# Scores and products with v share three PSUM slots; the softmax denominator is applied on the way out of PSUM; q and k load through a ring of three

## The chip, the cores and the metric

One kernel, one launch, on one core of a Trainium2 chip. The metric is device time in microseconds, so less is better. One core has five engines that run side by side and wait for each other by semaphores: TensorE (PE, its weight loads are shown apart as PEld), VectorE (DVE), ScalarE (ACT), GpSimd (POOL) and SyncE (SP), which here issues all DMAs.

## What is computed

Attention with rotary positions over 4 batches of 8 heads, 576 positions, 64 dimensions a head, and two feed-forward layers behind it, of 2304 tokens, 512 to 2048 to 512 channels. The first has a rational function between its two products, the second a squared relu.

```python
q_rot, k_rot = (rotate(q), rotate(k))
scores = scale * np.matmul(q_rot, k_rot.transpose(0, 1, 3, 2))
scores = scores - np.max(scores, axis=-1, keepdims=True)
attn = np.exp(scores)
attn = attn / (np.sum(attn, axis=-1, keepdims=True) + 1e-09)
x = np.matmul(attn, v)
...
h = x @ w_in
P = a[0] + a[1] * h + a[2] * h * h + a[3] * h * h * h
Q = 1.0 + np.abs(b[0]) * np.abs(h) + np.abs(b[1]) * h * h
x = (P / (Q + 1e-06)) @ w_out
...
h = np.maximum(x @ w2_in, 0.0)
out = (h * h) @ w2_out
```

## The kernel before

The kernel has two stages. The attention works on 16 pairs of heads, and a pair in five units (c = 0 to 4) of 128 query rows of each of its two heads (the last unit holds the 64 rows that are left). The feed-forward stage, called MoE in the code, then runs 160 steps, each 12 products into `ph` (two splits of x by two splits of the weights, three of the four, for each of four slices) and 12 products into the output banks.

**A pair, engine by engine.** `rope` loads q and k of a pair into `raw` (one DMA for q, one for k). POOL multiplies by the table of cosines and sines, adds the two halves, ACT casts the high part (`qh`, `kh`), POOL subtracts to get the low part (`ql`, `kl`). `scores` makes 12 matmuls for a unit, six for each head, into the two PSUM tiles `sc0` and `sc1` (two banks each). DVE takes each tile out with one instruction that writes `e` and the row minimum of the negated scores (`neg`), which frees the tile. ACT takes the exponential and sums the row (`sums`). PE transposes `e` into two PSUM banks (`tr`), from which ACT and DVE copy to `et`. `av` multiplies `et` by v, in two parts of 256 and 320 query columns, into two PSUM banks (`y`). DVE copies each part into the SBUF tile `t`. `normalise` adds 1e-9 to the sums on DVE, takes the reciprocal and a transpose there, sends the row to DRAM (`dr`) and back as three broadcast loads (`rr`). POOL multiplies `t` by `rr` into `xf`, the input of the feed-forward stage.

**What sets the order.** Each operation is a task with an engine, a cost in nanoseconds and a rank (position in the program plus an offset by kind from the table `RANK`). `Plan.run` simulates the engines with these costs and, each time an engine is free, takes the task with the smallest rank among those that are ready; a bonus `BOND` keeps tasks of one PE layout together. The instructions are then written in that order, so each engine works through a fixed list, and its first waiting instruction holds up all behind it. A task depends on another through keys (`r`, `w`). In the kernel before, the key of a score tile is `("sc", h)`, the one of a product with v `("y", i)`:

```python
self.pe(6 * 131, (n, "qk"), product, r=rd, w=[("sc", h) for h in range(2)], mode="rows")
```

so a unit's 12 score matmuls wait until both tiles of the unit before have been taken out. The eight PSUM banks are `sc0` and `sc1` (two each), `tr` (two) and `y` (two); in the feed-forward stage the last four are the output banks, and the first four `ph`.

The weights of the feed-forward stage are unpacked in chunks, each a DMA, three instructions on DVE (`wy`), two on ACT (`wx`, and the cast to `wsi`, `wso`, `wli` or `wlo`) and one on POOL; six chunks are unpacked while the attention still runs.

Of the kernel before, what the change touches and what calls it, by code (L numbers as in the profile page):

```python
# [9 lines left out]
F32 = mybir.dt.float32  # L10
# [4 lines left out]
ALU = mybir.AluOpType  # L15
# [4 lines left out]
P = 128  # L20
# [20 lines left out]
TRANSPOSE = 60  # L41
# [52 lines left out]
class Plan:  # L94
# [7 lines left out]

    LATENCY = {"dma": 2000}

    def __init__(self):
        self.tasks, self.writer, self.readers, self.base = [], {}, {}, 0
        self.order = set()

    def add(self, eng, ns, rank, fn, r=(), w=(), after=(), mode="", shared=False):
# [15 lines left out]
        self.order.update((d, i) for d in late)  # L125

# [6 lines left out]
    def run(self, trace=True):  # L133
# [13 lines left out]
        self.seq = [0] * len(tasks)  # L147
# [27 lines left out]
SWITCH, BOND = 160, 77.2  # L175

RANK = {"const": -332.5, "load": -240.8, "rope": 66.7, "add": -190.1, "hi": 466.7, "lo": -245, "wrap": 223.7,
        "spread": -16.2, "vload": -62.2, "qk": 7.4, "max": -58.9, "exp": 101.9, "dup": 356, "tr": -448.9,
        "trc": 381.9, "eth": -54.1, "av": 438, "t": 370.8, "inv": 804, "fin": -323.6, "wload": 966,
        "wx": 467.4, "wy": 51.1, "wh": 143.9, "wl": -174.2, "xh": 554.7, "xl": 53.4, "h": -384.7,  # L180
        "chain": -206.7, "gh": -85.2, "gl": 575.4, "o": 40.3, "evac": -273.4, "out": -182.5}


class Ops:
# [5 lines left out]
    def pe(self, ns, rank, fn, r=(), w=(), mode="full"):  # L190
        self.plan.add("pe", ns, rank, fn, r, w, mode=mode)
# [16 lines left out]
    def tt(self, eng, n, rank, out, a, b, op, r=(), w=(), ps=False):  # L208
        ns = 150 + 2.2 * n if eng == "pool" else 68 + 1.042 * n
        self.plan.add(eng, ns, rank, lambda: self.engine(eng).tensor_tensor(ap(out), ap(a), ap(b), op=op), r, w,  # L210
                      shared=not ps)
# [6 lines left out]
    def ts(self, eng, n, rank, out, a, s0, s1, op0, r=(), w=(), ns=None, ps=False, **kw):  # L218
        ns = ns or (327 + 0.833 * n if eng == "pool" else 68 + 0.522 * n)
        self.plan.add(eng, ns, rank, lambda: self.engine(eng).tensor_scalar(  # L220
            ap(out), ap(a), ap(s0), ap(s1), op0=op0, **{k: ap(x) for k, x in kw.items()}), r, w, shared=not ps)
# [15 lines left out]
class Attention(Ops):  # L237


    def __init__(self, nc, plan, early, late, scores, banks, dram, qk, v, tables, ident, xf):  # L240
# [3 lines left out]
        self.sc, self.tr, self.y = scores.ring(2, [P, 2, 512], F32, "sc"), banks[:2], banks[2:]  # L244
        self.ny = 0
        self.tab = early.tile([P, 2, S], F32, "tab")
        self.raw = early.tile([P, 4, S], F32, "raw")
# [7 lines left out]
        self.t = late.tile([P, S], F32, "t")  # L255
        self.rr = late.tile([P, S], F32, "rr")
        self.dr = [dram.tile([32, 4, 32], F32, name=f"dr{i}") for i in range(2)]

    def constants(self):
        for i, cols in enumerate((slice(0, KCUT), slice(KCUT, S))):  # L260
            self.dma((40 * i, "const"), self.tab[:, :, cols], self.tables_ap[:, :, cols], w=[("tab", i)], ns=900)
        self.dma((90, "const"), self.ident, self.ident_ap, w=["ident"])

    def rope(self, p):
        raw, b, at = self.raw, p % 2, 9 * (p - 1)
# [29 lines left out]
    def scores(self, p, c):  # L295
# [11 lines left out]
        def product():  # L307
            for i in range(3):
                for j in range(2):
                    for h, (rows, m, terms) in enumerate(jobs):  # L310
                        w, k = terms[i]
                        self.mm(self.sc[h][m, j, 0:288], w[rows], k[rows, 288 * j:288 * j + 288], i == 0, i == 2)

        self.pe(6 * 131, (n, "qk"), product, r=rd, w=[("sc", h) for h in range(2)], mode="rows")

    def unit(self, p, c):
# [9 lines left out]
        for h, rows, i, col in [(0, every, 0, c), (1, every, 1, 5 + c)] if c < 4 else [(h, slice(64 * h, 64 * h + 64), 1, 4) for h in range(2)]:  # L326

            self.ts("dve", 2 * 288, (n + h, "max"), e[rows, i].rearrange("p (j k) -> p j k", j=2), self.sc[h][rows, :, 0:288],
                    -SCALE, None, ALU.mult, op1=ALU.min, accum_out=self.neg[b][rows, col:col + 1], ns=760, ps=True,
                    r=[("sc", h), "scores"], w=[("neg", b, col, h), ("e", slot, h)])  # L330
# [56 lines left out]
    def av(self, p, part):  # L387
        n = (256, 320)[part]
        b = p % 2
        at = 9 * p + 5 * part  # L390
        y = self.y[self.ny % len(self.y)]
        yk = ("y", self.ny % len(self.y))
        self.ny += 1
# [4 lines left out]
        def product(js):  # L398
            for j in js:
                for h in range(2):  # L400
                    kc, slot = (4 * h + j, 4 * h + j) if j < 4 else (8, 8 + h)
                    self.mm(y[64 * h:64 * h + 64, 0:n], self.vst[b][:, slot], self.et[part][b][:, kc, :], j == 0, j == 4)

        for i, js in enumerate(AVCUT):
            self.pe((5 + 1.667 * n) * len(js), (at + 0.5 * i, "av"), lambda js=js: product(js),
                    r=keys + [("v", b), "early"], w=[yk], mode="columns")
        self.take("dve", n, (at, "t"), self.t[:, 256 * part:256 * part + n], y[:, 0:n], r=[yk], w=[("t", part)])

    def normalise(self, p):
        b = p % 2  # L410
        at = (9 * p, "inv")
        r, rt, dr, rr = self.r[b], self.rt[b], self.dr[b], self.rr
        self.ts("dve", 32, at, r, self.sums[b], 1e-9, None, ALU.add,
                r=[("sum", b, i) for i in range(9)] + [("sums", b)], w=[("r", b)])
        self.plan.add("dve", 270, at, lambda: self.nc.vector.reciprocal(ap(r), ap(r)), w=[("r", b)])
        self.plan.add("dve", 100, at, lambda: self.nc.vector.transpose(out=ap(rt), in_=ap(r)), r=[("r", b)], w=[("rt", b)])
# [3 lines left out]
        for h, first, src, n in ((0, 0, 0, S), (1, 0, S + 64, 512), (1, 512, S, 64)):  # L420
            self.dma(at, rr[64 * h:64 * h + 64, first:first + n], row[src:src + n].unsqueeze(0).to_broadcast([64, n]),
                     r=[("dr", b)], w=[("rr", h, first)])
        bb, hp = divmod(p, NHP)
# [18 lines left out]
class Weights(Ops):  # L442
# [15 lines left out]
    def chunk(self, i, rank):  # L458
# [7 lines left out]
        self.dma(at("wload"), self.raw, self.chunks[i], r=[("xf", 1)] if i < WFIRST else [], w=[raw], ns=1500)  # L466
# [9 lines left out]
class Moe(Ops):  # L476
    def __init__(self, nc, plan, early, late, hidden, banks, xf, weights, a, b, out):
# [12 lines left out]
        self.ps_o = banks  # L490
        self.before = {("o", i): (("tr", "y")[i // 2], i % 2) for i in range(4)}
# [23 lines left out]
    def split_x(self, b, dm, at):  # L515
# [3 lines left out]
        pairs = {("xf", NHP * t + dm) for t in range(STARTS[b] // S, (STARTS[b] + n - 1) // S + 1)}  # L519
# [3 lines left out]
    def unit(self, i):  # L523
# [51 lines left out]
        for dm in range(NDM):  # L575
# [6 lines left out]
            was = [("xf", NHP * t + dm) for t in range(B)] if m == g == 0 else []  # L582
# [119 lines left out]
```

## Time and profile before

| | us |
|---|---|
| median of 3 runs | 1116.99 |
| lowest, highest run | 1111.1, 1119.37 |
| the profiled execution, its own time | 1115.98 |
| its span in the trace | 1114.2 |
| first score matmul of the second pair (pair 1) | 33.15 |
| first score matmul of the last pair (pair 15) | 274.92 |
| first product into `ph` | 297.92 |

A stretch of the trace is read by the busy time of each engine in it, by what ended the idle time of an engine, and by the granted clock of TensorE as a share of its full 2.4 GHz. PE's busy time is modelled and counts matmuls that wait in its pipeline, so a busy PE isn't PE at its peak.

### The profile page before, as it was taken

How to read it: one execution, taken by the hardware profiler on the slowest of the kernel's cores; microseconds unless marked ns; L12 is line 12 of the kernel's file. 1: busy time of each engine (PE TensorE's matmuls, PEld its weight loads, DVE VectorE, ACT ScalarE, POOL GpSimd, SP SyncE). 2: the span in 40 equal slices, each digit the busy share in tenths (PEclk: the TensorE clock that was granted, in tenths of full speed). 3: DMA queues.
4: the chain of work that ended last, by engine and by line, in shares of the span. 5: the costliest groups of instructions: out<-in, count | busy, mean ns of one | idle time of the engine just before them, and what ended most of it. 6: DMA issues, size and time to landing. Idle time of an engine off the chain costs nothing.

```text
span 1114.2 us, 17891 instructions
## 1 busy us (share of the span) xinstructions
PE 1061.9 (95%) x6752; PEld 901.6 (81%) x6752; DVE 794.3 (71%) x1487; ACT 621.8 (56%) x1187; POOL 535.3 (48%) x431
## 2 busy tenths in 40 slices
PE   4998889899889999999999999999999999999998
PEld 3666666666678888888888889888888888888887
DVE  5779888877699888997998899863254446444434
ACT  4667767766668876775766677553443224223221
POOL 4867887872267877877886768320020002001000
PEclk9989989989989999999999999999999999999999
DMA  5344443331001111111110200230021003000002
GB/s 165 119 146 137 128 149 121 111 120 37 23 19 39 53 43 58 36 41 39 57 39 20 76 1 20 76 114 20 1 76 58 20 23 110 1 20 1 35 35 102
DMA packets 26823, 69.19 MB, mean 62 GB/s; under 512 B 6384, under 2 KB 10608, under 8 KB 26736
## 3 DMA queue, kind: packets, MB, share of 16 engines
q1 hardware_dynamic: 26736, 68.04, 19.7%
q8 instruction: 53, 0.87, 0.3%
q14 instruction: 34, 0.28, 0.1%
HBM read 63.05 MB, written 4.98 MB: 61 GB/s over the span
## 4 chain that ended last, share of the span: by engine, by line
PE 87%; DVE 8%; issue 2%; DMA 1%; ACT 1%; POOL 1%; SPq 0%; DVEq 0%; ACTq 0%; POOLq 0%
PE bank L234 42%; PE ph L234 35%; PE sc L234 6%; DVE e L220 4%; PE bank L372 3%; DVE et L385 1%; DMA raw<-in_qk 1%; DVE r L220 1%; POOL raw L210 0%; ACT e L200 0%; DVE wy L215 0%; SPq L231 0%; DMA cols<-in_b 0%; DVE xl L210 0%; POOL ql L210 0%
## 5 line engine op out<-in xcount | busy, mean ns | idle before, releaser
L234 PE MATMUL ph<-xh,wsi 128*128 128x464 f32 (+1 forms) x680 | 199.1, 374 | 4.5 <-DVE g L215 4.5
L234 PE MATMUL bank<-gh,wso 128*128 128x464 f32 (+1 forms) x680 | 197.6, 372 | 0.0
L198 ACT CAST gh<-g 128x464 fp32r<-128x464 f32 (+1 forms) x160 | 92.0, 577 | 153.1 <-PE bank L234 147.7
L234 PE MATMUL bank<-gh,wlo 128*128 128x464 f32 (+1 forms) x600 | 174.3, 371 | 0.0
L234 PE MATMUL ph<-xh,wli 128*128 128x464 f32 (+1 forms) x600 | 174.0, 371 | 0.0
L210 DVE TENSOR_TENSOR gl<-g,gh 128x464 fp32r<-128x464 f32 (+1 forms) x80 | 53.9, 674 | 150.1 <-ACT gh L198 150.0
L234 PEld LDWEIGHTS ph<-xh,wsi 128*128 128x128 f32 x680 | 128.2, 189 | 21.4 <-ACT tt L200 4.8
L234 PEld LDWEIGHTS bank<-gh,wso 128*128 128x128 f32 x680 | 127.6, 188 | 14.8
L220 DVE TENSOR_SCALAR_CACHE_REDUCE e<-sc 128x576 f32<-128x576 f32 (+1 forms) x160 | 115.5, 751 | 26.9 <-PE sc L234 22.7
L200 ACT ACTIVATE e<-e,neg 128x576 f32<-128x576 f32 x144 | 110.9, 773 | 39.5 <-DVE e L220 39.4
L234 PE MATMUL ph<-xl,wsi 128*128 128x464 f32 (+1 forms) x340 | 127.1, 374 | 0.5 <-DVE xl L210 0.5
L234 PE MATMUL bank<-gl,wso 128*128 128x464 f32 (+1 forms) x340 | 126.5, 372 | 0.0
L234 PEld LDWEIGHTS ph<-xh,wli 128*128 128x128 f32 x600 | 112.6, 188 | 13.3
L234 PEld LDWEIGHTS bank<-gh,wlo 128*128 128x128 f32 x600 | 112.6, 188 | 12.9
L210 POOL TENSOR_TENSOR gl<-g,gh 128x464 fp32r<-128x464 f32 (+1 forms) x80 | 103.1, 1290 | 24.9 <-ACT gh L198 20.1
L234 PE MATMUL bank<-gl,wlo 128*128 128x464 f32 (+1 forms) x300 | 111.6, 372 | 0.0
L234 PE MATMUL ph<-xl,wli 128*128 128x464 f32 (+1 forms) x300 | 111.4, 371 | 0.0
L210 POOL TENSOR_TENSOR u<-u,ab 128x464 f32<-128x464 f32 (+1 forms) x80 | 100.1, 1254 | 3.3
L234 PE MATMUL bank<-et,vst 128*64 128x256 f32 (+1 forms) x640 | 100.4, 440 | 0.9 <-DVE et L385 0.9
L210 DVE TENSOR_TENSOR xf<-bank,xf 128x464 f32<-128x464 f32 (+1 forms) x120 | 74.4, 635 | 34.9 <-PE bank L234 34.0
L234 PE MATMUL sc<-kh,qh 64*128 64x288 f32 (+1 forms) x320 | 60.6, 379 | 37.7 <-DVE e L220 25.1
L200 ACT ACTIVATE tt<-ph 128x464 f32<-128x464 f32 (+1 forms) x80 | 44.3, 555 | 91.0 <-DVE g L210 81.6
(68 smaller groups left out, 2007.9 us busy)
## 6 DMA issues: line engine op xcount, KB each, us to landing
raw<-in_qk SPq DMA_DIRECT2D x30, 576.0 KB
rawi<-in_wi SPq DMA_DIRECT2D x32, 512.0 KB
rawo<-in_wo SPq DMA_DIRECT2D x32, 512.0 KB
vst<-in_v SPq DMA_DIRECT2D x16, 320.0 KB
out<-xf SPq DMA_DIRECT2D x12, 232.0 KB
rr<-dr SPq DMA_DIRECT2D x16, 144.0 KB
rr<-dr SPq DMA_DIRECT2D x16, 128.0 KB
out<-xf SPq DMA_DIRECT2D x8, 228.0 KB
```

Of the source, the lines that this page charges most:

```text
L198: self.nc.scalar.copy(ap(out), ap(src))
L200: self.nc.scalar.activation(ap(out), ap(src), func, **{k: ap(x) for k, x in kw.items()})
L210: self.plan.add(eng, ns, rank, lambda: self.engine(eng).tensor_tensor(ap(out), ap(a), ap(b), op=op), r, w, shared=not ps)
L220: self.plan.add(eng, ns, rank, lambda: self.engine(eng).tensor_scalar(ap(out), ap(a), ap(s0), ap(s1), op0=op0, **{k: ap(x) for k, x in kw. ...
L234: self.nc.tensor.matmul(ap(out), ap(w), ap(x), start=start, stop=stop)
L372: self.nc.tensor.transpose(ap(self.tr[i])[0:src.shape[1], 64 * k:64 * k + 64], src[rows], ap(self.ident)[rows, rows])
L385: self.plan.add("dve", 68 + 1.042 * n, rank, lambda: self.nc.vector.tensor_copy(ap(out), ap(src)), r, w)
```

## The change

Three things change in the attention, and the order of nearly everything with them. First, PSUM: `sc0`, `sc1` and a third tile of two banks (`bank2`, which holds what were the two `y` banks) are three equal slots. A score task takes any two (`grab`), DVE's eviction gives one back (`drop`). A product with v takes one for both of its halves, and gives it back when DVE has read it. The planner hands out the slots as it goes, and may hold an engine idle for up to 800 ns for a task of smaller rank. Second, `av` now needs `rr`: DVE multiplies the product in PSUM by `rr` straight into `xf`, so that the copies to `t` and POOL's multiplication go away, and 1e-9 is added on ACT and not on DVE. `av` comes in three pieces for each part as before, but all of it is placed after the pair's reciprocal, so in the pair that follows. Third, `raw` is a ring of three tiles for q and k, not one tile for each. In the feed-forward stage a planner's delay of 130 ns between PE tasks falls away, so the order of its products changes too, from groups of three to groups of twelve. Number, shape and operands of the products are the same.

```diff
-    def add(self, eng, ns, rank, fn, r=(), w=(), after=(), mode="", shared=False):
+        self.where, self.slots, self.patient = {}, {}, 0
+    def add(self, eng, ns, rank, fn, r=(), w=(), after=(), mode="", shared=False, grab=(), drop=(), only=None):
...
+        vacant, last = dict.fromkeys(range(NSLOT), 0.0), {}
+        def able(i):
+            grab, _, only = self.slots.get(i, ((), (), None))
+            if not grab:
+                return ready_at[i]
+            times = sorted(t for s, t in vacant.items() if only is None or s == only)
+            return max(ready_at[i], times[len(grab) - 1]) if len(times) >= len(grab) else math.inf
-            start, eng = min((max(free[e], min(ready_at[i] for i in q)), e) for e, q in open_.items() if q)
-            i = min((i for i in open_[eng] if ready_at[i] <= start),
-                    key=lambda i: (tasks[i][2] - BOND * (tasks[i][5] == mode), i))
+            wait = {i: max(0, able(i) - start) for i in open_[eng]}
+            i = min((i for i, t in wait.items() if t <= HOLD * (i < self.patient)),
+                    key=lambda i: (tasks[i][2] - BOND * (tasks[i][5] == mode) + PULL * wait[i], i))
+            start += wait[i]
...
+            for x in grab:
+                s = min((s for s in vacant if only is None or s == only), key=lambda s: (vacant[s], s))
+                del vacant[s]
+                self.where[x] = s
...
+            for x in drop:
+                s = self.where[x]
+                vacant[s], last[s] = end + CROSS, i
...
-                wait = 0 if (i, u) in self.order else self.LATENCY.get(eng) or (SAME if same else CROSS)
+                wait = 0 if (i, u) in self.order else self.LATENCY.get(eng) or (SAME * (eng != "pe") if same else CROSS)
...
-RANK = {"const": -332.5, "load": -240.8, "rope": 66.7, "add": -190.1, "hi": 466.7, "lo": -245, "wrap": 223.7,
...
+HOLD, PULL = 800, 0.2958
+RANK = {"on": -34.47, "const": 59.32, "load": 145.37, "rope": 96.23, "add": 57.15, "hi": 268.98,
...
-        self.sc, self.tr, self.y = scores.ring(2, [P, 2, 512], F32, "sc"), banks[:2], banks[2:]
...
+        self.ps, self.tr = scores.ring(NSLOT - 1, [P, 2, 512], F32, "sc") + [banks[2]], banks[:2]
...
-        self.raw = early.tile([P, 4, S], F32, "raw")
+        self.raw = early.ring(NRAW, [P, 2, S], F32, "raw")
...
+            i = (2 * p + j) % NRAW
+            raw, (hi, lo) = self.raw[i], parts[j]
...
-        self.pe(6 * 131, (n, "qk"), product, r=rd, w=[("sc", h) for h in range(2)], mode="rows")
+                        self.mm(self.slot(("sc", p, c, h))[m, j, 0:288], w[rows], k[rows, 288 * j:288 * j + 288], i == 0, i == 2)
+        keys = [("sc", p, c, h) for h in range(2)]
+        self.pe(6 * 131, (n, "qk"), product, r=rd, w=keys, mode="rows", grab=keys, after=self.before)
+        self.before = keys[:1]
+    def slot(self, key):
...
-                    r=[("sc", h), "scores"], w=[("neg", b, col, h), ("e", slot, h)])
+                    r=[key, "scores"], w=[("neg", b, col, h), ("e", slot, h)], drop=[key])
...
+        yk = ("y", p, part)
+        rr = [("rr", b, 0, 0), ("rr", b, 1, 0), ("rr", b, 1, 512)]
+        r, only = ([], NSLOT - 1) if p == NPAIR - 1 else (["scores"], None)
         keys = [("m", c, r) for c in ((0, 1), (2, 3, 4))[part] for r in range(2)] + [("c", r) for r in range(2)]
...
-            self.pe((5 + 1.667 * n) * len(js), (at + 0.5 * i, "av"), lambda js=js: product(js),
-                    r=keys + [("v", b), "early"], w=[yk], mode="columns")
-        self.take("dve", n, (at, "t"), self.t[:, 256 * part:256 * part + n], y[:, 0:n], r=[yk], w=[("t", part)])
+            self.pe((5 + 1.667 * n) * len(js), (at + AVSTEP * (3 * part + i), "on" if i else "av"), lambda js=js: product(js),
+                    r=keys + [("v", b), "early", *rr] + r, w=[yk], mode="columns", grab=[yk] * (i == 0), only=only)
+        bb, hp = divmod(p, NHP)
+        first = 256 * part
+        self.tt("dve", n, (at + 5 * part, "fin"), self.xf[:, hp, bb * S + first:bb * S + first + n],
+                Ref(lambda: ap(self.slot(yk))[:, 0, 0:n]), self.rr[b][:, first:first + n], ALU.mult,
+                r=rr + [yk] + r, w=[("xf", p, part)], ps=True, drop=[yk])
...
-        self.ts("dve", 32, at, r, self.sums[b], 1e-9, None, ALU.add,
-                r=[("sum", b, i) for i in range(9)] + [("sums", b)], w=[("r", b)])
...
+        self.act(32, at, r, self.sums[b], func=AF.Identity, bias=self.eps, sb=True,
+                 r=[("sum", b, i) for i in range(9)] + [("sums", b), "eps"], w=[("r", b)])
+        self.plan.add("dve", 370, at, lambda: self.nc.vector.reciprocal(ap(r), ap(r)), w=[("r", b)])
+        self.plan.add("dve", 130, at, lambda: self.nc.vector.transpose(out=ap(rt), in_=ap(r)), r=[("r", b)], w=[("rt", b)])
...
-        self.tt("pool", S, (9 * p, "fin"), self.xf[:, hp, bb * S:bb * S + S], self.t, rr, ALU.mult,
-                r=[("rr", 0, 0), ("rr", 1, 0), ("rr", 1, 512), ("t", 0), ("t", 1)], w=[("xf", p)])
...
-                if c == 1:
-                    self.av(p, 0)
+            self.normalise(p)
+            self.av(p, 0)
             self.av(p, 1)
-            self.normalise(p)
...
-        self.ps_o = banks
...
+        self.ps_o = banks[:2] + [banks[2][:, i] for i in range(2)]
...
-        banks = [ps.tile([P, 512], F32, name=f"bank{i}") for i in range(4)]
+        banks = [ps.tile(s, F32, name=f"bank{i}") for i, s in enumerate([[P, 512]] * 2 + [[P, 2, 512]])]
```

DVE in the middle of the attention: evictions of score tiles (`e,neg<-...`), copies to `et`, unpacking of weights (`wy`), and the work on sums and products. Before, in a row:

```order
L385 COPY et01_105<-bank0_64 128x2x64
L385 COPY et01_105<-bank1_65 128x2x64
L220 TENSOR_SCALAR e3_95,neg1_97<-sc0_123 64x576
L220 TENSOR_SCALAR e3_95,neg1_97<-sc1_124 64x576
L385 COPY et11_107<-bank1_65 128x8x64
L385 COPY t_108<-bank2_66 128x256
L385 COPY t_108<-bank3_67 128x320
L220 TENSOR_SCALAR e0_92,neg0_96<-sc0_123 128x576
L220 TENSOR_SCALAR e0_92,neg0_96<-sc1_124 128x576
L220 TENSOR_SCALAR wy_70<-rawo_72 128x512
L220 TENSOR_SCALAR r1_101<-sums1_99 128x32
```

The same place of a pair in the changed kernel:

```order
L253 TENSOR_SCALAR e2_93,neg0_95<-bank2_66 128x576
L253 TENSOR_SCALAR e2_93,neg0_95<-sc0_125 128x576
L253 TENSOR_SCALAR e3_94,neg0_95<-sc1_126 128x576
L253 TENSOR_SCALAR e3_94,neg0_95<-bank2_66 128x576
L428 COPY et00_103<-bank1_65 128x8x64
L253 TENSOR_SCALAR e0_91,neg0_95<-sc0_125 64x576
L253 TENSOR_SCALAR e0_91,neg0_95<-sc1_126 64x576
L428 COPY et00_103<-bank0_64 128x2x64
L428 COPY et00_103<-bank1_65 128x2x64
L243 TENSOR_TENSOR xf_67<-bank2_66,rr1_108 128x256
L428 COPY et10_105<-bank1_65 128x8x64
L463 RECIPROCAL r0_99<-r0_99 128x32
```

The copies to `t` and the addition to the sums are gone, a product with `rr` has come, the slots rotate, and the reciprocal stands right ahead of the next pair's first evictions.

POOL in the middle of the attention, before: the product by the table (`raw<-raw,tab`), the addition, the low parts, a chunk of weights and the product `xf<-t,rr`.

```order
L210 TENSOR_TENSOR raw_114<-raw_114,tab_113 128x1152
L210 TENSOR_TENSOR wsi1_74<-wy_70,wsi1_74 128x512
L210 TENSOR_TENSOR raw_114<-raw_114 128x576
L210 TENSOR_TENSOR raw_114<-raw_114,tab_113 128x1152
L210 TENSOR_TENSOR xf_68<-t_108,rr_109 128x576
L210 TENSOR_TENSOR ql1_87<-raw_114,qh1_86 128x576
L210 TENSOR_TENSOR raw_114<-raw_114 128x576
```

The changed kernel, one pair on POOL:

```order
L243 TENSOR_TENSOR ql0_118<-raw0_114,qh0_117 128x576
L262 MEMSET sums0_97 128x32
L243 TENSOR_TENSOR kl0_120<-raw1_115,kh0_119 128x576
L243 TENSOR_TENSOR raw0_114<-raw0_114,tab_113 128x1152
L243 TENSOR_TENSOR raw0_114<-raw0_114 128x576
L243 TENSOR_TENSOR raw1_115<-raw1_115,tab_113 128x1152
L243 TENSOR_TENSOR raw1_115<-raw1_115 128x576
```

`xf` has left POOL, and the buffer `raw0` that `ql0` has read is loaded anew and used two instructions later.

PE at the end of the attention, before: the last transposes, the products with v of the last pair (`vst1`), and the first products of the feed-forward stage.

```order
L372 MATMUL bank0_64<-ident_91,e3_95 64x64
L372 MATMUL bank1_65<-ident_91,e3_95 128x64
L234 MATMUL bank3_67<-et11_107,vst1_90 64x320 x10
L234 MATMUL ph0_3636<-xh0_3703,wsi0_73 128x464 x2
L234 MATMUL ph0_3636<-xl0_3704,wsi0_73 128x464
```

The changed kernel there:

```order
L415 MATMUL bank0_64<-ident_90,e3_94 64x64
L415 MATMUL bank1_65<-ident_90,e3_94 128x64
L268 MATMUL bank2_66<-et10_105,vst0_121 64x320 x2
L268 MATMUL bank2_66<-et01_104,vst1_89 64x256 x10
L268 MATMUL bank2_66<-et11_106,vst1_89 64x320 x10
L268 MATMUL ph0_3646<-xh0_3691,wsi0_72 128x464 x2
L268 MATMUL ph0_3646<-xl0_3692,wsi0_72 128x464
```

Both parts of the last pair's product with v, which now need that pair's `rr`, stand together ahead of the feed-forward stage.

## Rows read from the trace of the kernel before

**Rows 1.** Windows: busy us (and instructions) of each engine, granted clock, DMA share.

```profile
core 0: us, PE busy (x) PEld busy (x) DVE busy (x) ACT busy (x) POOL busy (x), PEclk, DMA share, GB/s
33.20:274.90 241.70, 217.00 (x2553) 152.86 (x2551) 201.35 (x512) 169.43 (x377) 175.74 (x115) 0.92 0.39 122
340.00:700.00 360.00, 360.00 (x1720) 322.06 (x1719) 324.44 (x513) 256.59 (x445) 272.84 (x245) 1.00 0.13 40
```

**Rows 2.** Timeline of PE: first score matmuls of pair 1 and of pair 15.

```profile
33.15 0.51 PE L234 MATMUL sc<-kh,qh 64*128 64x288 f32 x4
34.12 0.65 PE L234 MATMUL bank<-et,vst 128*64 128x256 f32 x4
...
274.92 0.53 PE L234 MATMUL sc<-kh,qh 64*128 64x288 f32 x4
```

**Rows 3.** Chain that ended last, 33.2 to 274.9, by engine and line.

```profile
by line: PE bank L234 26.2%; PE sc L234 24.0%; DVE e L220 15.2%; PE bank L372 13.7%; issue 6.0%; DVE et L385 5.2%; DVE r L220 3.0%; ACT e L200 1.8%; DVE wy L215 1.4%; ACT et L198 1.0%; DVE r L415 0.7%; DVE wy L220 0.6%; ACT kh L198 0.4%; AC
```

**Rows 4.** Waits, 33.2 to 274.9: total us, times, longest.

```profile
PE sc L234 <- DVE e L220: 21.3, 41, 1.9
...
DVE e L220 <- PE sc L234: 15.1, 25, 1.9
```

**Rows 5.** Timeline of DVE and PE around one unit's scores.

```profile
107.95 0.76 DVE L220 TENSOR_SCALAR_CACHE_REDUCE e<-sc 128x576 f32<-128x576 f32 x1
...
108.77 0.40 PE L234 MATMUL sc<-kh,qh 64*128 64x288 f32 x1 [0.85 <-DVE e L220]
...
109.45 0.52 PE L234 MATMUL sc<-kh,qh 64*128 64x288 f32 x3 [0.28 <-DVE e L220]
```

**Rows 6.** Groups of POOL by shape, 33.2 to 274.9: busy us, mean ns, idle before.

```profile
L210 POOL TENSOR_TENSOR raw<-raw,tab 128x1152 f32<-128x1152 f32 x26 | 69.1, 2665 | 18.6 <-DMA raw<-in_qk 18.4
L210 POOL TENSOR_TENSOR raw<-raw 128x576 f32<-128x576 f32 x27 | 39.4, 1472 | 0.4
L210 POOL TENSOR_TENSOR xf<-t,rr 128x576 f32<-128x576 f32 x14 | 20.4, 1459 | 23.1 <-DVE t L385 21.0 <-DMA rr<-dr 1.6 <-DVE r L415 0.6
L210 POOL TENSOR_TENSOR kl<-raw,kh 128x576 fp32r<-128x576 f32 x14 | 20.2, 1442 | 5.3 <-ACT kh L198 5.3
L210 POOL TENSOR_TENSOR ql<-raw,qh 128x576 fp32r<-128x576 f32 x14 | 19.9, 1418 | 9.0 <-ACT qh L198 9.0
L210 POOL TENSOR_TENSOR wsi<-wy,wsi 128x512 fp32r<-128x512 f32 x3 | 3.8, 1279 | 0.0
```

**Rows 7.** Timeline of SP and POOL: two raw loads issued, the first one used.

```profile
174.65 1.72 SPq L231 DMA_DIRECT2D raw<-in_qk  x2
...
178.41 2.65 POOL L210 TENSOR_TENSOR raw<-raw,tab 128x1152 f32<-128x1152 f32 x1 [2.40 <-DMA raw<-in_qk]
```

**Rows 8.** Groups of DVE by shape, 33.2 to 274.9.

```profile
L385 DVE COPY et<-bank 128x512 f32<-128x512 f32 x28 | 19.3, 690 | 13.4 <-PE bank L372 10.8 <-ACT e L200 2.2
L220 DVE TENSOR_SCALAR r<-sums 128x32 f32<-128x32 f32 x14 | 14.7, 1047 | 2.8 <-ACT e L200 2.7
...
L385 DVE COPY t<-bank 128x320 f32<-128x320 f32 x14 | 6.8, 487 | 1.1
...
L385 DVE COPY t<-bank 128x256 f32<-128x256 f32 x14 | 5.9, 419 | 0.2
```

**Rows 9.** The page's groups: the nearest product of a PSUM bank and SBUF.

```profile
L210 DVE TENSOR_TENSOR xf<-bank,xf 128x464 f32<-128x464 f32 (+1 forms) x120 | 74.4, 635 | 34.9 <-PE bank L234 34.0
```

**Rows 10.** Timeline of SP and POOL: the reciprocals' way through DRAM, one pair.

```profile
198.26 0.57 SPq L231 DMA_DIRECT2D dr<-rt  x1
200.30 2.46 SPq L231 DMA_DIRECT2D rr<-dr  x3
...
204.79 1.42 POOL L210 TENSOR_TENSOR xf<-t,rr 128x576 f32<-128x576 f32 x1 [1.06 <-DMA rr<-dr]
```

**Rows 11.** Timeline of DVE, SP and PE at the end of the attention.

```profile
291.54 0.18 DVE L220 TENSOR_SCALAR r<-sums 128x32 f32<-128x32 f32 x1 [0.27 <-ACT e L200]
...
292.38 0.56 SPq L231 DMA_DIRECT2D dr<-rt  x1
...
294.75 3.24 PE L234 MATMUL bank<-et,vst 128*64 128x320 f32 x20 [0.93 <-DVE et L385]
297.92 0.69 PE L234 MATMUL ph<-xh,wsi 128*128 128x464 f32 x2
```

More of the change, by code (lines that the diff above doesn't have):

```diff
@@ L40 @@
 KCUT = 288
-TRANSPOSE = 60
+TRANSPOSE = 62
+NSLOT = 3
+AVSTEP = 1.5
+NRAW = 3
 ROPE = {(0, 0): "pool", (0, 1): "dve", (1, 0): "dve", (1, 1): "dve"}
@@ L125, in add @@
         self.order.update((d, i) for d in late)
+        if grab or drop:
+            self.slots[i] = (grab, drop, only)
     def barrier(self, fn, w):
@@ L174 @@
 SAME, CROSS = 130, 180
-SWITCH, BOND = 160, 77.2
-RANK = {"const": -332.5, "load": -240.8, "rope": 66.7, "add": -190.1, "hi": 466.7, "lo": -245, "wrap": 223.7,
[L178 to L181, printed above, removed]
+HOLD, PULL = 800, 0.2958
+SWITCH, BOND = 160, 58.5
+RANK = {"on": -34.47, "const": 59.32, "load": 145.37, "rope": 96.23, "add": 57.15, "hi": 268.98,
+        "lo": -35.36, "wrap": 223.7, "spread": -16.2, "vload": 194.98, "qk": 1.33, "max": -47.2,
+        "exp": 61.91, "dup": 356, "tr": -110.97, "trc": -329.26, "eth": -8.01, "av": 145.83, "t": 370.8,
+        "inv": 1.98, "fin": -54.52, "wload": 951, "wx": 502.88, "wy": 99.07, "wh": -102.22, "wl": -100.64,
+        "xh": 325.05, "xl": 106.51, "h": -619.65, "chain": -139.29, "gh": -154.06, "gl": 943.18, "o": 135.54,
+        "evac": -499.48, "out": -89.96}
 class Ops:
@@ L188, in __init__, with pe @@
         self.nc, self.plan = nc, plan
-    def pe(self, ns, rank, fn, r=(), w=(), mode="full"):
-        self.plan.add("pe", ns, rank, fn, r, w, mode=mode)
+    def pe(self, ns, rank, fn, r=(), w=(), mode="full", **kw):
+        self.plan.add("pe", ns, rank, fn, r, w, mode=mode, **kw)
     def act(self, n, rank, out, src, r=(), w=(), func=AF.Copy, sb=False, extra=0, **kw):
@@ L216, in stt, with ts @@
             ap(out), ap(a), ap(s), ap(b), op0=op0, op1=op1), r, w, shared=not ps)
-    def ts(self, eng, n, rank, out, a, s0, s1, op0, r=(), w=(), ns=None, ps=False, **kw):
+    def ts(self, eng, n, rank, out, a, s0, s1, op0, r=(), w=(), ns=None, ps=False, drop=(), **kw):
         ns = ns or (327 + 0.833 * n if eng == "pool" else 68 + 0.522 * n)
         self.plan.add(eng, ns, rank, lambda: self.engine(eng).tensor_scalar(
-            ap(out), ap(a), ap(s0), ap(s1), op0=op0, **{k: ap(x) for k, x in kw.items()}), r, w, shared=not ps)
+            ap(out), ap(a), ap(s0), ap(s1), op0=op0, **{k: ap(x) for k, x in kw.items()}), r, w, shared=not ps,
+                      drop=drop)
     def copy(self, eng, n, rank, out, src, r=(), w=()):
@@ L254, in __init__ @@
         self.et = [late.ring(2, [P, 9, n], F32, f"et{i}") for i, n in enumerate((256, 320))]
-        self.t = late.tile([P, S], F32, "t")
-        self.rr = late.tile([P, S], F32, "rr")
+        self.rr = late.ring(2, [P, S], F32, "rr")
+        self.eps = late.tile([P, 1], F32, "eps")
         self.dr = [dram.tile([32, 4, 32], F32, name=f"dr{i}") for i in range(2)]
@@ L465, in chunk @@
         at = lambda kind: (rank + self.lag, kind)
-        self.dma(at("wload"), self.raw, self.chunks[i], r=[("xf", 1)] if i < WFIRST else [], w=[raw], ns=1500)
+        self.dma(at("wload"), self.raw, self.chunks[i], r=[("xf", 1, 1)] if i < WFIRST else [], w=[raw], ns=1500)
         self.act(DM, at("wx"), x, high.bitcast(F32), r=[raw], w=["wx"], sb=True, scale=2.0 ** -112)
@@ L488, in __init__ @@
         self.ps_h = hidden.ring(4, [P, 512], F32, "ph")
-        self.ps_o = banks
-        self.before = {("o", i): (("tr", "y")[i // 2], i % 2) for i in range(4)}
+        self.ps_o = banks[:2] + [banks[2][:, i] for i in range(2)]
+        self.before = {("o", i): ("tr", i) if i < 2 else ("y", NPAIR - 1, 1) for i in range(4)}
         cols = early.tile([P, 16], F32, "cols")
@@ L518, in split_x @@
         n = BLOCKS[b]
-        pairs = {("xf", NHP * t + dm) for t in range(STARTS[b] // S, (STARTS[b] + n - 1) // S + 1)}
+        pairs = {("xf", NHP * t + dm, i) for t in range(STARTS[b] // S, (STARTS[b] + n - 1) // S + 1) for i in range(2)
+                 if STARTS[b] < S * t + (256, S)[i] and STARTS[b] + n > S * t + (0, 256)[i]}
         self.act(n, (at, "xh"), xh, src, r=[("acc", b, dm), "late" if b else "m_early", *pairs], w=[("xh", b, dm)], sb=True)
@@ L581, in unit @@
             ps, dst = self.ps_o[dm][:, 0:n], self.xf[:, dm, sl]
-            was = [("xf", NHP * t + dm) for t in range(B)] if m == g == 0 else []
+            was = [("xf", NHP * t + dm, i) for t in range(B) for i in range(2)] if m == g == 0 else []
             if g == 0:
```

50 lines of the change are left out of this document (25 added, 25 removed).

## The prediction

> **What bounds the kernel now.** I read the windows first. From 340 us on PE is busy in every microsecond at the full granted clock, with 1720 matmuls in 360 us, 0.2093 us each [rows 1]. The feed-forward stage has 3840 such products, 804 us at that rate, and the change alters neither their number nor their shape; it can win only in the attention. There the first score matmuls of pair 1 and pair 15 stand 274.92 - 33.15 = 241.8 us apart [rows 2], so a pair takes 17.27 us. No engine is full in that stretch: DVE 201 of 242 us, POOL 176, ACT 169, and PE, whose busy time is modelled, 217 at a mean granted clock of 0.92 (so some of it at the lower of the two levels) [rows 1]. The chain that ended last passes through PE's scores (24%) and DVE's evictions (15%) in turn [rows 3]. The waits say why: PE stood idle 21.3 us, in 41 waits, for DVE to take out scores, and DVE 15.1 us for PE to make them [rows 4]. One such turn: DVE's first eviction starts at 107.95, the next unit's matmuls into that tile at 108.77 after 0.85 us idle, those into the other tile at 109.45 after another 0.28 [rows 5].
>
> The second thing to see is POOL. In the same stretch it waited 21.0 us ahead of its product with the reciprocals for DVE's copies to `t`, 18.4 us for raw q and k, and 9.0 and 5.3 us for ACT's casts [rows 6]. Its list is fixed, so a late product with `rr` holds up the rotary work of later pairs.
>
> **The change part by part**, against the profiled execution's own 1115.98 us (the median of the runs, 1116.99, is 1.0 above it).
>
> *Three slots.* A unit may start its scores when one old tile and the third slot are free, so a wait like that one ends one eviction earlier. At most it gives back the whole 21.3 us [rows 4], at least the share of the units in which no product with v holds the third slot: by the order two of five units of a pair stand between a product's first matmul and its reading, so three fifths, 12.8 us. A unit's scores (0.97 us from 33.15 to 34.12 [rows 2]) and two evictions of 0.76 [rows 5] make 2.5 us even without overlap, 12.5 us for five. So the slots alone would allow 12.5 us a pair, and something else ends last: POOL, below.
>
> *Product with v times `rr` from PSUM.* DVE's two copies of 0.419 and 0.487 us go [rows 8], two products of the same sizes come. The nearest row is a PSUM tile and an SBUF tile of 464 columns at 0.635 us [rows 9]; the two copies differ by 1.06 ns a column, so at 256 and 320 columns it is 0.41 and 0.48. I take no difference; if each cost the full 0.635 it would be 0.36 us a pair, 5 us in all on an engine with slack. POOL loses 1.459 us a pair and the wait for `t` ahead of it, 21.0 / 14 = 1.5 us [rows 6].
>
> *1e-9 on ACT.* On DVE this instruction of 32 columns took 1.047 us on average [rows 8], and 0.18 at the end of the attention, when POOL is through [rows 11]: most of it is waiting inside the instruction. It is 3.0% of the chain, 7.3 us [rows 3]. ACT has 72 us to spare [rows 1]; no row shows a like instruction on it, so between nothing and the 0.18 us of DVE's, covered by that slack. The Trainium skill ("SBUF — State Buffer", "Who interferes with whom") says that such a plain tensor-scalar of SBUF data can be shut out by a running GpSimd instruction, and that an instruction with a single SBUF input isn't; by that rule the new product from PSUM, with `rr` as its one SBUF input, would not be stretched either. The 1.047 against 0.18 agrees.
>
> *Ring of three.* q of a pair can now be rotated before the low parts of the pair ahead are made. But by the order POOL still makes both low parts and then at once multiplies the tile whose load may only be issued when the first low part has been made. That is what happened before: loads issued at 174.65, the first used at 178.41, 2.40 us idle [rows 7]. So this wait stays once a pair.
>
> *POOL's period.* Two products by the table, two additions and two low parts are 2 x 2.665 + 2 x 1.472 + 1.418 + 1.442 = 11.13 us [rows 6]. Add 2.40 for the load [rows 7], the waits for ACT as before, (9.0 + 5.3) / 14 = 1.02, and four chunks of weights that by the order still lie among the rotary work, 4 x 1.279 / 14 = 0.37 [rows 6]. That is 14.9 us. DVE's busy time without the instruction that moves to ACT is (201.4 - 14.7) / 14 = 13.3 us a pair [rows 1, 8], so POOL ends last. The pair goes from 17.27 to 14.92: 14 x 2.35 = 32.9 us gained.
>
> *Products wait for `rr`.* In the middle this is covered. From the sums to `rr` it takes 0.84 us to the first DMA [rows 11], 2.04 to the second and 4.49 to its use [rows 10], 7.4 us. The order puts a pair's product behind the scores of units 1 to 4 of the next pair, at least three fifths of a period, 9 us. Without that cover each pair would pay what is missing, with the transposes and scores behind it on PE. On SP the loads of `rr` stand behind one raw load that waits for POOL's second low part; a late POOL delays them, 1.6 us of margin.
>
> At the end nothing covers it: both products of pair 15 now stand ahead of the feed-forward products on PE. Before, from the sums' instruction to the first feed-forward product it was 297.92 - 291.54 = 6.4 us [rows 11]. Now it is 7.4 us plus the 20 matmuls, 3.2 us [rows 11], 10.6: a loss of 4.2 us. DVE's list also has chunks of weights there, which may add up to 3. The skill ("DMA: Bandwidth & Descriptors", "Latency and other measured facts") gives a DMA a fixed cost of about 2 us, most of it the receipt from memory. By that figure two hops would be 4 us, not the 6.5 measured [rows 10], and the loss about 1.7; the rows decide, since here three loads are issued one behind the other.
>
> *Order of the feed-forward products.* PE is full in that stage [rows 1], and a matmul's price is that of its columns. Of the 816 us from the first product to the span's end 12 aren't products; I take 0, with 4 either way.
>
> Sum: 1115.98 - 32.9 + 4.2 = 1087.3; I say 1088.
>
> **The rivals.** *POOL doesn't hold it up*: if raw loads come earlier than I think, DVE's 13.3 us a pair is the limit: 1115.98 - 14 x 3.97 + 4.2 = 1065. For it: POOL may run ahead of the pairs by up to a pair. Against it: before, the same order of instructions waits [rows 7].
>
> *The slots give only the units without a product*: the third slot is occupied when it's wanted, and POOL's relief isn't on the path: 1115.98 - 12.8 + 4.2 = 1107. For it: only the chain's 24% and 15% [rows 3] speak of scores, and POOL's idle time counts only where PE waits for q or k, which the waits don't show [rows 4]. Against it: the moved sums alone are another 7.3 us of the chain.
>
> *The reciprocal becomes a wait*, and the kernel slower. It now stands on DVE right ahead of the next pair's evictions, and needs ACT's new instruction, which stands behind the last exponential and a cast of q that waits for POOL. Before, DVE waited 0.27 us there at the end [rows 11] and 2.8 us in all [rows 8]. Two copies, a product and one copy of 0.69 [rows 8] stand between, so a small delay is covered. If it stalls DVE by w each pair, 14 w is lost; from w = 28.7 / 14 = 2.0 us the gain is gone, and from 2.8 us the kernel is over 1% slower. At 3 us a pair: 1115.98 - 28.7 + 42 = 1129. Against it: POOL's additions for that cast come almost a period earlier.
>
> **How the numbers follow.** The bound between change and no change is 1% here, 11 us (the runs before spread over 8). Forecast, about 1076 to 1100: 0.56. DVE's limit, 1062 to 1076: 0.18. Slots alone, 1100 to 1112: 0.16, of which a third is under 1105.8. The reciprocal's wait: 0.10, of it 0.08 over 1128. That gives faster 0.78, same 0.14, slower 0.08. The range goes from DVE's limit, 1064, to the case of the slots alone with the 4 us of the last stage, 1111.
>
> **What would show it.** Right: the first scores of pairs 1 and 15 some 209 us apart; PE's wait for evictions under 9 us; no row for copies to `t` nor for POOL's product with `rr`; POOL's first product by the table after two low parts still idle for its load; about 10 us between the last sums' instruction and the first feed-forward product; that stage within 4 us. Wrong: DVE's reciprocal with idle time for ACT ahead of it; PE's products with v waiting for `rr` in the middle; or POOL without a wait for raw data while another engine's list sets the pair.

## The result

The changed kernel takes 1087.6 us (median of four runs, 1086.6 to 1088.2) against 1116.8 before: ratio 0.974 [0.971, 0.978]. The forecast was 1088. The total fits by luck: four terms were off and cancel. By the spans of the two profiled executions:

| us | before | after | difference | forecast |
|---|---|---|---|---|
| start to first scores of pair 1 | 33.15 | 30.84 | -2.3 | 0 |
| from there to those of pair 15 | 241.77 | 197.61 | -44.2 | -32.9 |
| from there to the first product into `ph` | 23.00 | 30.50 | +7.5 | +4.2 |
| from there to the end | 816.28 | 827.05 | +10.8 | 0 |
| span | 1114.20 | 1086.00 | -28.2 | -28.7 |

The runs below were timed in three further sets. In these the kernel before took 1112.0, 1112.7 and 1115.2 us (medians), and the changed kernel wasn't timed again; so a difference of 1 to 3 us between two runs is a hint, unless their traces show it.

### The profile page after: what moved, and what is told of

Read it like the earlier page. It is cut to its first block, busy times and chain, and to the rows that moved or that the text cites. A ratio compares the mean times of both kernels' runs of the same rounds, so it can differ in the third digit from the quotient of the medians.

```text
span 1086.0 us, 17812 instructions
## 1 busy us (share of the span) xinstructions
PE 1049.9 (97%) x6752; PEld 886.4 (82%) x6752; DVE 773.8 (71%) x1471; ACT 617.2 (57%) x1203; POOL 507.2 (47%) x416
## 3 DMA queue, kind: packets, MB, share of 16 engines
q1 hardware_dynamic: 26736, 68.04, 20.3%
## 4 chain that ended last, share of the span: by engine, by line
PE 88%; DVE 7%; issue 2%; ACT 1%; DMA 1%; POOL 1%; SPq 0%; DVEq 0%; POOLq 0%
PE bank L268 41%; PE ph L268 35%; PE sc L268 9%; PE bank L415 3%; DVE e L253 2%; DVE et L428 1%; DMA raw<-in_qk 1%; DVE xf L243 0%; POOL raw L243 0%; DVE wy L248 0%; DVE xl L243 0%; ACT tt L233 0%; DVE wy L253 0%; SPq L265 0%; DVE g L243 0%
## 5 line engine op out<-in xcount | busy, mean ns | idle before, releaser
L268 PEld LDWEIGHTS bank<-gh,wlo 128*128 128x128 f32 x600 | 111.9, 188 | 16.8 <-DVE xf L243 3.6
L243 POOL TENSOR_TENSOR u<-u,ab 128x464 f32<-128x464 f32 (+1 forms) x80 | 102.4, 1284 | 2.3
L253 POOL TENSOR_SCALAR u<-ab,cols 128x464 f32<-128x464 f32 (+1 forms) x80 | 62.9, 787 | 76.6 <-DVE g L248 53.3
L243 POOL TENSOR_TENSOR raw<-raw,tab 128x1152 f32<-128x1152 f32 (+2 forms) x30 | 77.4, 2580 | 39.2 <-DMA raw<-in_qk 39.2
L253 DVE TENSOR_SCALAR_CACHE_REDUCE e<-sc 128x576 f32<-128x576 f32 (+1 forms) x108 | 79.2, 749 | 5.9 <-PE sc L268 4.4
```

The source lines that it names most:

```text
L268: self.nc.tensor.matmul(ap(out), ap(w), ap(x), start=start, stop=stop)
```

## The profile after

Windows of the changed kernel, the first from pair 1 to pair 15 [rows 1]:

```profile
core 0: us, PE busy (x) PEld busy (x) DVE busy (x) ACT busy (x) POOL busy (x), PEclk, DMA share, GB/s
30.80:228.50 197.70, 191.90 (x2507) 138.55 (x2503) 169.79 (x484) 166.29 (x382) 148.80 (x96) 1.00 0.46 139
340.00:700.00 360.00, 357.31 (x1687) 315.02 (x1687) 321.50 (x496) 236.69 (x419) 245.94 (x222) 1.00 0.14 42
```

A pair takes 14.12 us, 14 times within 0.5. PE's idle time fell from 24.7 to 5.8 us, and its busy time from 217.0 to 191.9. The granted clock is now 1.00, before 0.92; the window also holds 46 matmuls fewer, 20 of them products with v (some 2.4 us) that now come after it. In the second window PE is no longer full: it makes 33 matmuls fewer.

Waits of that stretch (total us, times, longest) [rows 4]; the weight loads' wait in the kernel before; then the chain of the changed kernel by line [rows 3]:

```profile
POOL raw L243 <- DMA raw<-in_qk: 29.4, 13, 3.4
...
PEld sc L268 <- DVE e L253: 10.0, 28, 1.0
...
PEld bank L268 <- DVE e L253: 5.2, 14, 1.0
...
PE sc L268 <- DVE e L253: 0.8, 2, 0.6
PE bank L268 <- DVE e L253: 0.7, 1, 0.7
```

```profile
PEld sc L234 <- DVE e L220: 34.8, 51, 2.4
```

```profile
by line: PE sc L268 41.2%; PE bank L268 21.9%; PE bank L415 15.7%; DVE e L253 11.8%; issue 4.9%; DVE et L428 4.3%; DVEq L253 0.1%
```

The matmuls' wait for evictions fell from 21.3 to 1.5 us, that of the weight loads from 34.8 to 15.2. POOL still waits for its raw data, for longer than before (18.4 us there). But nothing of POOL is on the chain: another engine's list sets the pair, which is half of a sign of being wrong that the prediction named (the other half, no such wait on POOL, didn't come). Groups by shape of the same stretch [rows 6, 8]:

```profile
L233 ACT ACTIVATE r<-sums,eps 128x32 f32<-128x32 f32 x14 | 4.5, 322 | 0.5
L463 DVE RECIPROCAL r<-r 128x32 f32<-128x32 f32 x13 | 4.5, 343 | 0.0
L243 DVE TENSOR_TENSOR xf<-sc,rr 128x320 f32<-128x320 f32 x8 | 3.9, 492 | 0.0
...
L243 DVE TENSOR_TENSOR xf<-bank,rr 128x256 f32<-128x256 f32 x5 | 2.1, 425 | 3.8 <-PE bank L268 3.8
```

The products from PSUM cost what the copies did (0.42 and 0.49 us, forecast 0.41 and 0.48); the reciprocal never waits for ACT.

## The experiments

**POOL.** Three runs keep the order of every engine and change what POOL does or waits for (the third changes DVE's part too). A fourth raw tile:

```diff
-self.raw = early.ring(NRAW, ...)    raw = self.raw[(2 * p + j) % NRAW]
+self.raw = early.ring(4, ...)       raw = self.raw[(2 * p + j) % 4]
```

> The changed kernel in the same order, with a fourth raw tile (the planner still counts three), so that a load may be issued one product by the table earlier and POOL's 2.4 us wait for it goes. Theory of the prediction, 'POOL ends last': the pair falls to DVE's 13.3 us or nearly, time 1073 to 1080. Rival 'PE's list': POOL only waits elsewhere (for ACT's casts, whose buffers PE frees); the period stays at 14.1, the time at 1085 to 1089.

1086.2 us, pairs of 14.1. POOL's groups, 101.1 to 214.3, of the changed kernel and then with four tiles:

```profile
L243 POOL TENSOR_TENSOR raw<-raw,tab 128x1152 f32<-128x1152 f32 x15 | 39.8, 2656 | 19.5 <-DMA raw<-in_qk 19.5
...
L243 POOL TENSOR_TENSOR ql<-raw,qh 128x576 fp32r<-128x576 f32 x9 | 12.8, 1426 | 2.2 <-ACT qh L231 2.2
L243 POOL TENSOR_TENSOR kl<-raw,kh 128x576 fp32r<-128x576 f32 x8 | 11.5, 1437 | 2.4 <-ACT kh L231 2.4
```

```profile
L243 POOL TENSOR_TENSOR raw<-raw,tab 128x1152 f32<-128x1152 f32 x15 | 42.6, 2839 | 2.1 <-DMA raw<-in_qk 1.9
...
L243 POOL TENSOR_TENSOR ql<-raw,qh 128x576 fp32r<-128x576 f32 x9 | 12.8, 1417 | 13.5 <-ACT qh L231 13.5
L243 POOL TENSOR_TENSOR kl<-raw,kh 128x576 fp32r<-128x576 f32 x8 | 11.3, 1412 | 7.9 <-ACT kh L231 7.9
```

The 17.6 us taken from the load came back as 16.8 us of waiting for ACT's casts. POOL runs ahead, and something else paces it: its lead (from the end of `kl` to the first scores of its pair) stays at 11.3 us. Then more load, an extra product into an unused tile:

```diff
+nc.gpsimd.tensor_tensor(dum, tab[:, 0], tab[:, 1], op=mult)   # ahead of ql, pairs 2 to 15
```

> The changed kernel, in the same order, with one more POOL product of 576 columns (some 1.46 us, into a tile that nobody reads) ahead of each pair's low part of q. Theory of the prediction, 'POOL ends last': each pair takes 1.4 us more, 14 times, the time goes to about 1108, the pairs to 15.6 us. Rival 'PE's list': POOL has some 2.5 us a pair to spare (its waits are for buffers that PE frees), the period stays at 14.1 to 14.4, the time at 1087 to 1092.

1098.4 us, between the two. Of the first seven pairs (31.1 to 131.5 us) five stay at 14.1 to 14.2 and two take 14.7 and 15.0, while POOL's lead falls from 11 to 5 us; the next seven average 15.6. POOL's groups, 116.6 to 225.8:

```profile
L243 POOL TENSOR_TENSOR raw<-raw,tab 128x1152 f32<-128x1152 f32 x14 | 37.1, 2647 | 18.1 <-DMA raw<-in_qk 18.1
...
L325 POOL TENSOR_TENSOR dum<-tab 128x576 f32<-128x576 f32 x7 | 10.8, 1544 | 0.0
L243 POOL TENSOR_TENSOR ql<-raw,qh 128x576 fp32r<-128x576 f32 x7 | 9.9, 1419 | 0.0
L243 POOL TENSOR_TENSOR kl<-raw,kh 128x576 fp32r<-128x576 f32 x7 | 9.9, 1416 | 0.0
```

With POOL last, its waits for ACT are 0.0 and the load's remains, 2.6 a pair. Its own cycle without the extra product is 15.6 - 1.5 = 14.1: as long as the pair in the changed kernel.

POOL's lateness doesn't reach the other engines through q and k, whose lead stays near 5 us, but through SP's list. The reciprocals' way to DRAM (`dr`) stands there behind a raw load that waits until POOL has made `ql`; the prediction had seen this, with 1.6 us of margin. DVE's wait in the same stretch, which the changed kernel has nowhere in the attention, and one such case on DVE, POOL and SP:

```profile
DVE xf L243 <- DMA rr<-dr: 16.3, 7, 3.4
```

```profile
198.24 0.21 DVE L473 STREAM_TRANSPOSE rt<-r 128x32 f32<-128x32 f32 x1
...
201.03 1.42 POOL L243 TENSOR_TENSOR ql<-raw,qh 128x576 fp32r<-128x576 f32 x1
...
202.47 0.33 SPq L265 DMA_DIRECT2D raw<-in_qk  x1
202.85 0.57 SPq L265 DMA_DIRECT2D dr<-rt  x1
```

`rt` is ready at 198.45 and leaves 4.4 us later. Undoing the real part:

```diff
-DVE: xf = y * rr
+DVE: t = copy(y);  POOL, after part 1: xf = t * rr
```

> The changed kernel in the same order, with the old way out of PSUM: DVE copies the product with v to an SBUF tile, POOL multiplies it by the reciprocals into xf. It undoes that part alone. POOL gets 1.46 us a pair and a wait for DVE in its list. By the run with an extra product on POOL (pairs of 15.5 us once its lead is used up) the time is 1098 or more, with the wait for DVE up to 1110. If POOL's load didn't count, 1086 to 1090.

1099.0 us and a like picture: 14.1 us for seven pairs, then some 15.5. Here DVE's copy also waits for POOL's product to have read `t` (12.1 us in seven waits, 116.6 to 225.8), since there is one such tile. So taking the product off POOL is worth some 11.4 us in this order, as a condition of the shorter period.

**1e-9 on DVE again**, same order:

```diff
-ACT: r = Identity(sums + eps)
+DVE: r = sums + 1e-9
```

> The changed kernel in the same order, with 1e-9 added on DVE again and not on ACT: that part alone undone. Theory 'PE's list': DVE has 1.5 us a pair to spare, an instruction of up to 1.05 us fits into it; pairs of 14.1 to 14.3 us, 1087 to 1090. Theory of the chain of before (3.0% of it was this instruction, 7.3 us): 1093 to 1095.

1089.9 us, pairs of 14.33: it is worth 2 to 3 us (14 times 0.21 in the pairs), not the 7.3 of the chain. The row there:

```profile
L467 DVE TENSOR_SCALAR r<-sums 128x32 f32<-128x32 f32 x14 | 8.8, 631 | 0.0
```

**Slots and order, two by two.** Each of these is planned anew:

```diff
-grab=keys                      (scores: any two slots; products with v: any)
+grab=keys, only=(0, 1)         (products with v: only slot 2)
```

> The changed kernel with scores held to the two old slots and products with v to the third; the order is planned anew under that limit, the rest of the change stays. Theory 'slots': the wait of scores for both old tiles is what the 17.3 us of a pair were made of; the period goes from 14.1 back to 16 to 17 us, the time to 1114 to 1128. Theory 'relief' (POOL's product and the sums' addition were what counted): the period stays at 14.1 to 14.9, the time under 1100.

```diff
-HOLD, PULL = 800, 0.2958
+HOLD, PULL = 0, 0.2958
```

> The changed kernel, all three slots shared, but the planner may no longer hold an engine idle for a task of smaller rank (800 ns before, 0 now), so that the attention is planned in another order. A control for the run with the slots apart, which was planned anew too. Theory 'slots': with three shared slots another order costs little; pairs of 14.1 to 15.5 us, time 1087 to 1106. Rival 'order': what counts is the order that the ranks were set for, and any other loses as much as the slots apart did (pairs of 18 us); over 1125.

> The run before this one with scores held to two slots and products with v to the third: the slots apart, in a second order. Theory 'slots': again 16.5 us a pair or more, 1118 or more. Rival 'order': the loss with the slots apart was that of one bad order; this one stays under 1112.

| pair, us (time) | planner holds 800 ns | holds nothing |
|---|---|---|
| slots shared | 14.12 (1087.6) | 20.3 (1172.2) |
| slots apart | 18.2 (1146.4) | 18.8 (1153.4) |

Theory 'slots' foresaw 16 to 17 us apart and 14.1 to 15.5 shared without holding; both came out slower, and shared slots in the other order are the slowest of all. Windows of 60 to 220 us, shared without holding, apart with, and the changed kernel:

```profile
60.00:220.00 160.00, 134.10 (x1438) 93.04 (x1438) 115.15 (x288) 101.89 (x228) 95.77 (x62) 0.83 0.38 122
```

```profile
60.00:220.00 160.00, 138.29 (x1633) 97.79 (x1629) 124.09 (x322) 114.09 (x255) 106.81 (x69) 0.93 0.42 132
```

```profile
60.00:220.00 160.00, 156.62 (x2060) 111.56 (x2055) 139.10 (x396) 135.92 (x312) 123.39 (x82) 1.00 0.47 142
```

Where PE idles more, 26 and 22 us against 3, the granted clock is lower too, 0.83 and 0.93 against 1.00. One fall in the second of these runs: from 94.0 to 101.0 us PE is idle for 2.6 us at a granted clock of 1.00, and from 101.0 to 104.4 the clock is at its lower level, 1.2 GHz (0.51). With these ranks the gain of the attention needs both, shared slots and an order that may hold an engine back; neither alone beats the 17.27 us of before. The ranks were the same in all four, so this is a verdict on these orders, not on every possible one. Nor are the slots apart the old PSUM: there the two parts of a product with v had a bank each, here they take turns in one slot, and what that costs wasn't tried. The ring of three was never undone by itself.

**The feed-forward stage.** The old order first (ranks and the 130 ns):

```diff
-SAME * (eng != "pe")
+SAME * (eng != "pe" or i >= self.patient)     # and the old ranks of h, o, chain, gh, gl, evac, ...
```

> The changed kernel with the old ranks of the feed-forward tasks and the old planner delay of 130 ns between PE tasks of that stage, so that its products alternate in groups of three again; the attention's order is the same. Theory 'order': the 10 us that the stage grew by (812.2 to 822.3 us from the first product into ph to the last matmul) come from the order alone; the stage returns to 812 within 2, and the time to about 1078. Rival 'something else of the change' (the four output banks now lie in three tiles, other engines are later): the stage stays at 820 to 824, the time at 1086 to 1089.

1088.3 us; its products stand mostly in groups of three again, and from the first to the last matmul it takes 825 us: the order isn't it. What the trace of the changed kernel shows is small gaps where weights are loaded for an output bank. Their row in the waits from 340 to 1060 us (it has none in the kernel before), and the timeline of one:

```profile
PEld bank L268 <- DVE xf L243: 9.1, 21, 0.7
```

```profile
423.53 1.19 DVE L243 TENSOR_TENSOR xf<-bank,xf 128x464 f32<-128x464 f32 x2
...
424.78 0.30 PEld L268 LDWEIGHTS bank<-gh,wlo 128*128 128x128 f32 x2 [0.41 <-DVE xf L243]
```

DVE takes out two banks in a row, and the weights of the next product into an output bank are loaded only when both are read. Output banks 2 and 3 are now halves of one tile, `bank2`. As tiles of their own:

```diff
-self.ps_o = banks[:2] + [banks[2][:, i] for i in range(2)]
+self.ps_o = banks + outs.ring(2, [P, 512], F32, "po")      # pool reopened after the attention
```

> The changed kernel with the third slot in a PSUM pool of its own, which after the attention is reopened as two separate tiles of one bank each: the four output banks are four tiles again, as before the change; the order on PE is the same. Theory 'shared tile': as halves of one tile, output banks 2 and 3 are waited for together (each block's first product into bank 2 waits until DVE has also read bank 3), which is most of the 10 us; the stage falls from 822 to 812 to 815 us, the time to 1077 to 1081. Rival 'other engines are late': the same waits stand there for single banks; the stage stays at 820 to 824, the time at 1085 to 1089.

1074.3 us, below the range that was expected; ratio to the kernel before, timed beside it at 1112.7, 0.969 [0.964, 0.975]. With the same groups of products on PE the stage takes 812.7 us to its last matmul (822.3 in the changed kernel, 812.2 before), and the wait for `xf` has no row. The shared tile is the cause of the 10 us of that stage, and this is the fastest version. Of the other 4 us between the two profiled executions, 2.7 come from the granted clock at the end of the attention, below.

**The end of the attention.** Timeline of the changed kernel [rows 11]:

```profile
242.24 0.32 ACT L233 ACTIVATE r<-sums,eps 128x32 f32<-128x32 f32 x1
...
246.11 1.75 SPq L265 DMA_DIRECT2D rr<-dr  x3
...
247.84 2.38 PE L268 MATMUL bank<-et,vst 128*64 128x256 f32 x20 [0.68 <-DVE xf L243]
...
252.48 0.43 DVE L253 TENSOR_SCALAR wy<-rawi 128x512 uint32<-128x512 uint32 x1 [2.02 <-POOL wso L243]
252.94 0.42 DVE L243 TENSOR_TENSOR xf<-bank,rr 128x256 f32<-128x256 f32 x1
...
253.42 5.60 PE L268 MATMUL bank<-et,vst 128*64 128x320 f32 x20 [3.20 <-DVE xf L243]
...
258.95 0.82 PE L268 MATMUL ph<-xh,wsi 128*128 128x464 f32 x2
```

The first 20 matmuls start while the loads of `rr` are being issued: only DVE's product needs `rr`. The second 20 wait for it because both parts use one slot, and DVE's product stands behind a chunk of weights that waits 2.02 us for POOL. They then ran at the lower clock (granted 0.50 from 253.42 to 258.95), 5.60 us. In the run with separate output tiles they waited as long, 3.21 us, but ran at 1.00 in 2.91 us: why the clock fell in one and not in the other no run shows. With a bank of its own for the second part:

```diff
-y = self.slot(("y", p, part))
+y = self.tr[1]                     # pair 15, part 1
```

> The changed kernel in the same order, with the second part of the last pair's product with v in a bank of its own (the second transpose bank) and not in the slot of the first part. Theory 'slot': the matmuls don't wait for the reciprocals themselves, only DVE's product does; what stopped PE for 3.2 us was that the second part needed the slot that DVE's product of the first part frees; without it PE runs through, and the stretch from pair 15's first scores to the first product into ph falls from 30.4 to 24 to 27 us, the time by 3 to 6 us. Theory of the prediction 'the products wait for the reciprocals': the second part waits as before, nothing changes.

```profile
246.39 5.07 PE L268 MATMUL bank<-et,vst 128*64 128x256 f32 x40 [0.68 <-DVE xf L243]
254.55 1.14 PE L268 MATMUL ph<-xh,wsi 128*128 128x464 f32 x2 [3.08 <-ACT xh L231]
```

All 40 run through, so the slot it was; but the stretch is still 27.5 us, and 1086.1 us (1083.4 to 1086.3) is hardly less, where 3 to 6 us had been expected: PE now waits 3.08 us for ACT's casts, which stand behind the weights on ACT. Then products ahead of the wait:

```diff
-r=keys + [("v", b), "early", *rr]
+r=keys + [("v", b), *["early"] * (p < NPAIR - 1), *rr]
```

> The changed kernel in which the product with v of the last pair no longer counts as a user of the first arena, so that the feed-forward stage's buffers open before it and 36 of its products stand on PE ahead of the last pair's products with v. Theory: the wait of pair 15 for its reciprocals is all that stretched the end (30.4 us from its first scores to the first product into ph, 23.0 before); 36 products of 0.21 us cover 7.6 us of it; the time falls by 5 to 8 us to 1080 to 1083. Rival: the first feed-forward products wait for their casts on ACT and DVE as long as for the reciprocals; under 2 us are gained, 1086 to 1088.

1085.1 us, 2.6 less. The first product into `ph` comes 18.9 us after pair 15's first scores, 11.6 earlier than in the changed kernel; but 40 products with v now lie behind it, and from 380 to 400 us PE is idle for 2.8 us, where it was full. Both mends:

> Both mends together: output banks 2 and 3 as tiles of their own (it gave 13 us) and 36 feed-forward products ahead of the last pair's products with v (it gave 2.6 us). If they add: 1071 to 1073. If the gain of the second was taken back by the shared tile in that run: 1067 to 1070. If the wait only moves to the casts: 1074 to 1075.

1074.6 us: nothing beyond the separate tiles. What holds up the end is the unpacking of weights on ACT, DVE and POOL as much as `rr`; which of them must move was not tried.

## Why the prediction was right in its number, and where not

- **The number was luck.** The pairs gained 11.3 us more than forecast and the start 2.3; the end lost 3.3 us more and the last stage 10.8. Of the signs of being right, the missing rows, PE's short wait for evictions and POOL's idle time for its load came. The distance of the first scores (197.6 us, not 209), the end (16.7 us from the last sums to the first feed-forward product, not 10) and the last stage (+10.8, not within 4) did not.
- **"So POOL ends last"** failed. The sum of 14.9 us took over POOL's waits for ACT (1.02 a pair), which are the waits of an engine that is ahead. Its own cycle is 14.1; taking its wait for raw data away gave nothing. By the chain it is PE's list, with its turns with DVE's evictions, that sets 14.12; no run shortens that list, so this is read and not tested. POOL is just behind: its relief was needed, as the two runs with more load show.
- **"The slots alone would allow 12.5 us a pair"** had the wrong sort of term: with these ranks slots give nothing without the holding order. The forecast gave neither the order nor the clock a price. Of the 44.0 us between the two windows, 18.9 are idle time of PE. The other 25.1 are busy time. An estimate from the granted clock of 0.92 over 241.7 us: the clock can be some 0.08 x 241.7 = 19 of them, if PE was busy whenever it was low. How much it is by itself stays open, since no run holds the clock fixed.
- **"Products wait for `rr`", covered in the middle, +4.2 at the end**: covered it was; at the end the matmuls don't wait for `rr` themselves but for the slot behind DVE's product, and the stretch grew by 7.5, of it some 2.7 by the clock of that execution.
- **"Order of the feed-forward products: 0"** was right about order, and some 10 of the 10.8 us lost came from a line that the prediction passed over: the output banks as halves of one tile.
- **1e-9 on ACT** took 0.32 us there (forecast 0 to 0.18), hidden; worth 2 to 3 us. **The reciprocal as a wait**, the slower rival, didn't occur: 0.0 us idle. The Trainium skill ("SBUF — State Buffer", "Who interferes with whom") says that a DVE instruction with at most one input from SBUF, outside the modes that use two ports, doesn't contend with GpSimd. The trace agrees for the product from PSUM: 0.42 and 0.49 us, what the copies took.

## What to carry to other kernels

A wait counts into an engine's cycle only if the engine is late: see whether its lead over its user is constant (then it is paced) or shrinks, and test with one load more and one wait less. Then follow by what way its lateness spreads: here by a DMA list that it shares with others, not by what it makes. Before giving a gain to a resource, take it away in two orders: here, with these ranks, resource and order were worth something only together. When buffers are joined for one stage, look at who uses them in the next: halves of one tile are waited for as one.

## What was not expected of the hardware

With a fourth raw tile POOL waited less for its loads, but its product by the table grew from 2.656 to 2.839 us on average; why was not tried. The addition of 1e-9, 32 columns on DVE, took 0.63 us on average in the new order and 1.05 in the old [rows 8]. After the same wait of 3.2 us at the end of the attention the granted clock was 0.50 in one execution and 1.00 in another.
